# Gated linear attention and a multiplicative feed-forward block: state, scores and values of a chunk in one block of 64x64 quarters

## The chip, the cores and the metric

The kernel runs on one core of one Trainium2 chip. The metric is the device time of one execution in microseconds (us); the time of a kernel is the median of several runs. A profile is one further execution, with its own time; its span, from the first to the last instruction, is what the trace divides.

## The reference

For each of 4 batches and 8 heads, a state of 48x48 is decayed row by row and added to, token by token; q reads it. The result, 3072 tokens by 384, goes through a feed-forward block whose two gates are multiplied.

```python
batch, n_heads, seq, head_dim = (4, 8, 768, 48)
state = np.zeros((B, H, D, D), dtype=np.float32)
for t in range(S):
    state = alpha[:, :, t, :, None] * state + np.einsum('bhd,bhe->bhde', k[:, :, t], v[:, :, t])
    y[:, :, t] = np.einsum('bhd,bhde->bhe', q[:, :, t], state)
...
x = np.ascontiguousarray(attn_out.transpose(0, 2, 1, 3)).reshape(B * S, H * D)
a = x @ w1
b = x @ w2
h = a * b @ w3
return (h @ w_out).astype(np.float32)
```

w1 and w2 are 384x1024, w3 is 1024x1024, w_out 1024x384. These four weights arrive in 64-bit floats and are taken apart on the chip.

## The kernel before, in words

**Chunks.** The 768 tokens of a batch are 6 chunks of 128 (C), so there are 24 chunks in all (N) and chunk n is the first of its batch where n % 6 is 0. A loop over n from 0 to 24 has one step for each chunk and one more. It is software-pipelined: step n transposes chunk n + 1, computes the scores of chunk n, finishes the output of chunk n - 1, decays chunk n + 2 and takes logarithms for chunk n + 4.

**One chunk.** `logs` takes the logarithm of alpha (ScalarE). `decays` (L333) sums it over the tokens by a matmul with a triangular matrix and takes two exponentials, the tile `e`. `decayed` (L357) multiplies k and q by them (VectorE, tile `qk`). `transposed` (L370) turns `qk` on TensorE, and ScalarE copies it to `qkT`, with head 2j + i of a pair j on the 64 partitions of half i. `scores` (L446) multiplies k by q within a chunk, and VectorE masks them with a bitwise and against the upper triangle (L457) into `ms`. The output y of a chunk is the state times q (`attend_state`, L463) plus the values times the masked scores (`attend`, L477). ScalarE copies y to the tile `x` (L489), which SyncE stores to DRAM (`xd`), two transfers a chunk (`store`, L301, L305). `outer` (L386) forms k times v for the state, and `advance` (L405) decays the state every second chunk on GpSimd (T, L412). The decay factors get to T by way of DRAM: GpSimd's queue stores single rows of `e` (`ends`, L352 and L354) and loads them back with values on partitions (`load_ends`, L362, tile `dec`).

**Quarters.** A matmul with at most 64 rows and at most 64 columns of weights uses one 64x64 quarter of TensorE's array; four such run beside each other. From chunk 8 on (`TURNED`, L81) `turned_scores` (L422) leaves out the part of the scores that the mask removes: per pair and half one matmul of 64 keys by 128 queries and one of 64 by 64. For that, half i = 1 keeps its keys in exchanged halves, and the values must be exchanged too: `turn_v` (L164, two copies on GpSimd, L167) writes `vt`. The first 64 queries' values (`attend_low`, L415) of chunk n - 1 go between the scores of chunk n; the other 64 queries' (L482) follow after the transposes, with all 128 rows. Chunks 0 to 7 use the plain form: L454 for the scores, L485 for the values. In both, the two halves i write banks of their own (`sc[i]`, `y[i]`).

**Around it.** Three chunks make a group g of 384 tokens. `load_x` loads a group's x from `xd`, `split_x` (L503) splits it into three parts on ScalarE (L507) and VectorE (L508, L509), and `gate` makes one of 8 column tiles of a times b by 18 matmuls per factor (L515), in fp32r. Gates of groups 0 to 4 fill up the steps from 6 on. Weights w1 and w2 are converted (`to_fp32`, L226) in the same steps. After the loop the other gates, the product of w3 with w_out and the final projection follow.

**Order.** The framework schedules each engine's instructions by the order of the program, with `after_marks` holding back what follows until a marked instruction has been issued. SyncE's queue issues the loads of alpha, k, q, v and weights and the stores of x and of the gates (L590) in one order; before the change, `store` stands first in a step from step 6 on. v of chunks 3 to 7 is loaded by GpSimd's queue (L159).

Of the kernel before, what the change touches and what calls it, by code (L numbers as in the profile page):

```python
# [12 lines left out]
I32 = mybir.dt.int32  # L13
# [35 lines left out]
def kernel(  # L49
# [31 lines left out]
    TURNED = 8  # L81
# [79 lines left out]
    def turned(n):  # L161
        return TURNED <= n < N

    def turn_v(n):  # L164
        if turned(n):
            for half in range(2):
                nc.gpsimd.tensor_copy(out=vts[n % 2][ds(DP * half, DP), :, 0:D],  # L167
                                      in_=st["v", n][ds(DP * (1 - half), DP), 1::2, 0:D])
# [19 lines left out]
    made = work.tile([C, 2, NP, C], FP32, tag="ms", name="ms")  # L188
    utri, after = made[:, 0, 0, :], made[:, 0, 1, :]
# [3 lines left out]
    keep = p1.tile([C, C], I32, name="keep")  # L193
    keep_turned = p1.tile([C, 2, DP], I32, name="keep_turned")
# [11 lines left out]
    nc.vector.tensor_scalar_mul(keep, utri, -1.0)  # L206
    keep_bc = keep[:, None, :].to_broadcast([C, NP, C])
    for half in range(2):
        nc.gpsimd.tensor_copy(out=keep_turned[ds(DP * half, DP), 1 - half], in_=keep[ds(DP * half, DP), ds(DP * half, DP)])
    nc.gpsimd.memset(keep_turned[DP:, 1], -1)  # L210
# [122 lines left out]
    def decays(n):  # L333
# [17 lines left out]
        if n in ends:  # L351
            mark["pool"] = nc.gpsimd.dma_start(out=ends[n][0:1], in_=e[0:1, 0]).ins  # L352
        if n + 1 in ends:
            mark["pool"] = nc.gpsimd.dma_start(out=ends[n + 1][1:2], in_=e[C - 1:C, 1]).ins  # L354
        load_ends(n)
# [6 lines left out]
    def load_ends(n):  # L362
        if n not in ends:
            return
        with nc.allow_non_contiguous_dma(reason="single values to partitions"):
            for i in range(2):
                nc.gpsimd.dma_start(out=decs[n // 2 % 2][ds(DP * i, D)].rearrange("d m j -> d (m j)"),
                                    in_=ends[n].rearrange("m (j i d) -> i d (m j)", i=2, d=D)[i])
# [36 lines left out]
    def advance(n):  # L405
# [4 lines left out]
        nc.gpsimd.tensor_mul(dec, d[:, 0, :], d[:, 1, :])  # L410
# [4 lines left out]
    def attend_low(n, jj, i, half):  # L415

        s, w = ds(DP * i, DP), (vts[n % 2] if i else st["v", n])
        h = half * NP // 2 + jj
        nc.tensor.matmul(st["y", n][0][i][ds(DP * half, DP), jj, 0:DP], w[s, h if i else 2 * h, :],  # L419
                         st["ms", n][s, i, h, 0:DP], start=(n % NCH == 0 and jj == 0), stop=True, skip_group_check=True)  # L420

    def turned_scores(n):  # L422

        qkT = st["qkT", n]
        sc = [bank().rearrange("p (j c) -> p j c", j=NP) for _ in range(2)]
        for j in range(NP):
            for part in range(2):
                for i in range(2):
                    r, t = ds(DP * i, D), slice(DP * part, C)
                    nc.tensor.matmul(sc[i][ds(DP * (part ^ i), DP), j, t], qkT[r, 0, j, ds(DP * part, DP)],  # L430
                                     qkT[r, 1, j, t], start=True, stop=True)
            if turned(n - 1):
                for i in range(2):
                    attend_low(n - 1, j % 2, i, i ^ (j < 2))
        ms = work.tile([C, 2, NP, C], FP32, tag="ms", name="ms")
        for i in range(2):
            r = ds(DP * i, DP)
            low, high = (keep_turned[r, 0], keep_turned[:, 1]) if i else (keep[r, 0:DP], keep[:, DP:])
            for x, mask, t in ((slice(DP * i, DP * (i + 1)), low, slice(0, DP)), (slice(0, C), high, slice(DP, C))):
                masked = nc.vector.tensor_tensor(ms[x, i, :, t].bitcast(I32), sc[i][x, :, t].bitcast(I32),  # L440
                                                 mask[:, None, :].to_broadcast([x.stop - x.start, NP, DP]),
                                                 op=ALU.bitwise_and)
        ends_of_part1[0] = mark["ms", n] = masked.ins
        st["ms", n] = ms

    def scores(n):  # L446
        if turned(n):
            return turned_scores(n)
        qkT = st["qkT", n]
        sc = [bank().rearrange("p (j c) -> p j c", j=NP) for _ in range(2)]  # L450
        for j in range(NP):
            for i in range(2):
                r = ds(DP * i, D)
                nc.tensor.matmul(sc[i][:, j, :], qkT[r, 0, j, :], qkT[r, 1, j, :], start=True, stop=True)  # L454
        ms = work.tile([C, 2, NP, C], FP32, tag="ms", name="ms")
        for i in range(2):
            masked = nc.vector.tensor_tensor(ms[:, i].bitcast(I32), sc[i].bitcast(I32), keep_bc, op=ALU.bitwise_and)  # L457
        ends_of_part1[0] = mark["ms", n] = masked.ins
        st["ms", n] = ms

    HP = NP // 2

    def attend_state(n):  # L463
        qkT = st.pop(("qkT", n))

# [221 lines left out]
    for n in range(N + 1):  # L689
        if not 1 < n < FIRST:  # L690
            store()
# [185 lines left out]
```

## Time and profile before

| | us |
|---|---|
| median of 3 runs (463.63 to 465.16) | 464.42 |
| the profiled execution | 464.49 |
| its span | 462.8 |
| loop over chunks, with what precedes it | 0 to 184.6 |
| first gate matmul (L515) | 57.7 |
| after the loop | 184.6 to 462.8 |
| TensorE busy | 446.9 |
| VectorE busy | 371.7 |
| ScalarE busy | 276.4 |
| GpSimd busy | 95.1 |
| granted TensorE clock | 1.000 |

In the page and the trace, PE is TensorE's matmul, PEld its weight loads, DVE VectorE, ACT ScalarE, POOL GpSimd and SP SyncE; a q after a name is that engine's queue of DMA issues. L12 is line 12 of the kernel. A line of the timeline has the start, the time until the last of the merged instructions ended, the engine, the line, what is written and read, the shape and the count; in brackets stands the idle time ahead of it and who ended it. A line of a group has the busy time in all, the mean of one in ns, and the idle time ahead with its releasers. One fp32 matmul is two instructions. Ends of matmuls are modelled and overlap their successors, so differences of starts are used.

### The profile page before, as it was taken

How to read it: one execution, taken by the hardware profiler on the slowest of the kernel's cores; microseconds unless marked ns; L12 is line 12 of the kernel's file. 1: busy time of each engine (PE TensorE's matmuls, PEld its weight loads, DVE VectorE, ACT ScalarE, POOL GpSimd, SP SyncE). 2: the span in 40 equal slices, each digit the busy share in tenths (PEclk: the TensorE clock that was granted, in tenths of full speed). 3: DMA queues.
4: the chain of work that ended last, by engine and by line, in shares of the span. 5: the costliest groups of instructions: out<-in, count | busy, mean ns of one | idle time of the engine just before them, and what ended most of it. 6: DMA issues, size and time to landing. Idle time of an engine off the chain costs nothing.

```text
span 462.8 us, 11150 instructions
## 1 busy us (share of the span) xinstructions
PE 446.9 (97%) x4296; PEld 423.2 (91%) x4296; DVE 371.7 (80%) x610; ACT 276.4 (60%) x544; POOL 95.1 (21%) x186
## 2 busy tenths in 40 slices
PE   4998999999999999999999999999999999999996
PEld 2675699898999989999999999999999999999996
DVE  2779997999979988999998999997542967776671
ACT  4685975767658563988875676764545443333430
POOL 6234232325414430121221201212010000000000
PEclk9999999999999999999999999999999999999999
DMA  9999999999999974466856446412115875665511
GB/s 173 254 208 228 261 224 192 248 209 219 184 227 193 234 165 138 130 224 212 235 178 196 146 128 177 149 52 86 51 48 153 243 210 180 186 178 159 166 51 52
DMA packets 148869, 80.37 MB, mean 174 GB/s; under 512 B 97392, under 2 KB 138608, under 8 KB 148816
## 3 DMA queue, kind: packets, MB, share of 16 engines
q1 hardware_dynamic: 143040, 64.44, 57.3%
q0 software_dynamic: 5776, 15.22, 11.0%
q8 instruction: 34, 0.56, 0.5%
q14 instruction: 19, 0.16, 0.1%
HBM read 57.58 MB, written 22.06 MB: 172 GB/s over the span
## 4 chain that ended last, share of the span: by engine, by line
PE 88%; DVE 4%; DMA 4%; ACT 2%; issue 1%; SPq 0%; DVEq 0%; ACTq 0%
PE bank L515 72%; DMA kq<-in_q_dram 3%; PE bank L381 3%; PE bank L430 3%; PE bank L482 2%; PE bank L474 2%; PE bank L340 1%; PE bank L393 1%; PE bank L346 1%; PE bank L454 1%; PE bank L343 1%; PE bank L419 1%; DVE qk L359 1%; DVE ms L457 1%; PE bank L485 1%
## 5 line engine op out<-in xcount | busy, mean ns | idle before, releaser
L515 PE MATMUL bank<-x,w 128*128 128x384 f32 x1152 | 210.2, 337 | 1.7 <-ACT qkT L383 1.1
L515 PEld LDWEIGHTS bank<-x,w 128*128 128x128 f32 x1152 | 200.2, 188 | 4.1 <-ACT qkT L383 1.4
L515 PE MATMUL bank<-w3o,ab 128*128 128x384 f32 x576 | 100.2, 336 | 0.0
L515 PEld LDWEIGHTS bank<-w3o,ab 128*128 128x128 f32 x576 | 99.9, 188 | 0.0
L540 ACT ACTIVATE bank<-bank 128x384 f32<-128x384 f32 x96 | 45.6, 476 | 43.4 <-PE bank L515 43.1
L524 ACT ACTIVATE t<-bank 128x384 f32<-128x384 f32 x64 | 31.9, 499 | 54.9 <-PE bank L515 54.9
L590 POOL DMA_DIRECT2D abd<-ab x45 | 25.8, 573 | 137.9 <-DVE ab L576 121.3
L383 ACT COPY qkT<-bank 128x512 f32<-128x512 f32 x48 | 26.2, 596 | 24.8 <-PE bank L381 24.8
L641 DVE TENSOR_TENSOR ab<-abl,ab 128x1024 fp32r<-128x1024 f32 x24 | 29.3, 1223 | 12.3 <-ACT ab L640 12.3
L640 ACT ACTIVATE ab<-abl 128x1024 fp32r<-128x1024 f32 x24 | 25.5, 1061 | 20.2 <-PE bank L515 18.4
L515 PE MATMUL bank<-wo,w3T 128*128 128x384 f32 x192 | 35.9, 334 | 0.0
L576 DVE TENSOR_TENSOR ab<-bank,r 128x384 f32<-128x384 f32 x44 | 24.1, 548 | 12.5 <-PE bank L515 6.3
L515 PEld LDWEIGHTS bank<-wo,w3T 128*128 128x128 f32 x192 | 33.5, 188 | 0.0
L249 ACT ACTIVATE power<-power,rebias 128x512 uint32<-128x512 uint32 (+1 forms) x36 | 25.3, 701 | 12.6 <-DVE power L248 12.4
L359 DVE TENSOR_TENSOR qk<-kq,e 128x768 f32<-128x768 f32 x24 | 23.1, 964 | 11.3 <-ACT e L350 7.9
L526 DVE SCALAR_TENSOR_TENSOR o<-bank,t 128x384 f32<-128x384 f32 x24 | 13.4, 557 | 23.0 <-issue 13.7
L642 DVE SCALAR_TENSOR_TENSOR ab<-ab,abl 128x1024 fp32r<-128x1024 f32 x24 | 29.2, 1217 | 0.0
L526 DVE SCALAR_TENSOR_TENSOR r<-bank,t 128x384 f32<-128x384 f32 x40 | 22.0, 550 | 6.8 <-PE bank L515 3.4
L251 DVE SCALAR_TENSOR_TENSOR mant<-mant,rest 128x512 f32<-128x512 uint32 (+1 forms) x36 | 23.4, 649 | 3.7 <-ACT rest L244 3.7
L252 DVE SCALAR_TENSOR_TENSOR power<-raw,power 128x512 uint32<-128x512 uint32 (+1 forms) x36 | 23.5, 653 | 2.4 <-ACT power L249 2.4
L253 DVE TENSOR_TENSOR mant<-mant,power 128x512 f32<-128x512 f32 (+1 forms) x36 | 23.6, 655 | 0.5
L244 ACT ACTIVATE rest<-raw 128x512 f32<-128x512 uint32 (+1 forms) x36 | 23.3, 649 | 0.0
(102 smaller groups left out, 675.2 us busy)
## 6 DMA issues: line engine op xcount, KB each, us to landing
abl<-abd SPq DMA_DIRECT2D x24, 512.0 KB, 4.7
abd<-ab POOLq DMA_DIRECT2D x45, 192.0 KB, 3.2
raw<-in_moe_w_dram SPq DMA_DIRECT2D x64, 128.0 KB, 3.4
raw<-in_moe_w_dram SPq DMA_DIRECT2D x12, 512.0 KB, 5.8
xT<-xd POOLq DMA_DIRECT2D x9, 576.0 KB, 4.7
kq<-in_k_dram SPq DMA_DIRECT2D x24, 192.0 KB, 5.2
kq<-in_q_dram SPq DMA_DIRECT2D x24, 192.0 KB, 5.4
xd<-x SPq DMA_DIRECT2D x48, 96.0 KB, 3.9
```

The source lines that it names most:

```text
L249: nc.scalar.activation(power, power, AF.Relu, scale=2.0 ** 23, bias=rebias)
L359: mark["qk", n] = nc.vector.tensor_mul(qks[n % 3][:, :, :, 0:D], st.pop(("kq", n)), st.pop(("e", n)).rearrange("p i (h d) -> p i h d", h=H ...
L383: mark["qkT", n] = nc.scalar.copy(qkT[:, :, :, ds(DP * half, DP)], tp[half]).ins
L515: nc.tensor.matmul(p, w[part][i], x[part][i], start=start and part == parts[0] and i == 0, stop=stop and part == parts[-1] and i == n - 1, ...
L524: nc.scalar.activation(t, p1, AF.Copy, scale=(1.0 + 1.0 / P) * scale)
L526: nc.vector.scalar_tensor_tensor(to, p2, scale, t, op0=ALU.mult, op1=ALU.add)
L540: nc.scalar.activation(p, p, AF.Copy, scale=1.0 + 1.0 / P)
L576: nc.vector.tensor_mul(ab, p, r[0])
L590: (nc.gpsimd if late else nc.sync).dma_start(out=abd[g][:, f, :], in_=ab)
L640: nc.scalar.activation(t[:, 0], ab, AF.Copy, scale=1.0 - 2.0 ** -13)
L641: nc.vector.tensor_sub(t[:, 1], ab, t[:, 0].bitcast(FP32))
L642: nc.vector.scalar_tensor_tensor(t[:, 2], t[:, 0].bitcast(FP32), -1.0 - 1.0 / P, ab, op0=ALU.mult, op1=ALU.add)
```

## The change

- State, scores and values of a step become one block, `attention` (L471 of the new kernel), with two streams of matmuls. One stream uses the off-diagonal quarters and writes one bank: state, values of the first 64 keys and values of the last 64 keys for the heads of pairs 0 to 2 (LQ = 3). The other uses the diagonal quarters: all scores of chunk n, and then pair 3 of chunk n - 1, in a bank of its own. The streams are interleaved by a count of columns.
- All chunks take this form, chunks 0 to 7 too, so all get the exchange `vt`, now of all values that the off-diagonal and diagonal quarters need.
- The scores lie in two banks by queries and keys, and two masks of 512 and 256 columns take the place of four (two in chunks 0 to 7). `keep` becomes one tile with a half of ones.
- y lies in two banks of three pairs and one pair: ScalarE's two copies are of 384 and 128 columns instead of 256 each, and x is stored in four transfers a chunk instead of two.
- On GpSimd, `turn_v` comes ahead of `advance`, and the transfers of the decays and T's products wait for it by a mark. `load_ends` moves from `decays` of step n to behind `advance` of the next step.
- From step 6 on `store` follows the loads of k, q and v, so that `load_x` is first in its step. `logs(4)` waits for the copies of y.

```diff
     def turn_v(n):
-        if turned(n):
-            for half in range(2):
-                nc.gpsimd.tensor_copy(out=vts[n % 2][ds(DP * half, DP), :, 0:D],
-                                      in_=st["v", n][ds(DP * (1 - half), DP), 1::2, 0:D])
+        if n < N:
+            for i in range(2):
+                mark["vt"] = nc.gpsimd.tensor_copy(out=vts[n % 2][ds(DP * i, DP), :, 0:D],
+                                                   in_=st["v", n][ds(DP * (1 - i), DP), i::2, 0:D]).ins
...
-        if n in ends:
-            mark["pool"] = nc.gpsimd.dma_start(out=ends[n][0:1], in_=e[0:1, 0]).ins
-        if n + 1 in ends:
-            mark["pool"] = nc.gpsimd.dma_start(out=ends[n + 1][1:2], in_=e[C - 1:C, 1]).ins
-        load_ends(n)
+        with after_marks("vt"):
+            if n in ends:
+                mark["pool"] = nc.gpsimd.dma_start(out=ends[n][0:1], in_=e[0:1, 0]).ins
+            if n + 1 in ends:
+                mark["pool"] = nc.gpsimd.dma_start(out=ends[n + 1][1:2], in_=e[C - 1:C, 1]).ins
...
+    def attend(n):
+        ms, vc, vt, qkT = st.pop(("ms", n)), st.pop(("v", n)), vts[n % 2], st.pop(("qkT", n))
+        y = [bank()[:, 0:x * C].rearrange("p (j c) -> p j c", c=C) for x in (LQ, NP - LQ)]
+        first, state = set(), n % NCH > 0
+        def add(j, i, w, x, t):
+            at = j >= LQ
+            to = y[at][ds(DP * (i if at else 1 - i), DP), j - LQ * at, t]
+            nc.tensor.matmul(to, w, x, start=(at, i) not in first, stop=True, skip_group_check=True)
+            first.add((at, i))
+        def steps(heads):
+            for j in heads * state:
+                yield 2, [(j, i, Ts[n % 2][ds(DP * i, D), j, :], qkT[ds(DP * i, D), 1, j, :], slice(0, C)) for i in range(2)]
+            for j in heads:
+                yield 2, [(j, i, vt[DP:, j, :] if i else vc[0:DP, 2 * j, :], ms[ds(DP * i, DP), 0:2, j, :], slice(0, C))
+                          for i in range(2)]
+            for j in heads:
+                yield 1, [(j, i, vc[DP:, 2 * j + 1, :] if i else vt[0:DP, j, :], ms[ds(DP * i, DP), 2, j, :], slice(DP, C))
+                          for i in range(2)]
...
+        def copied():
+            x = work.tile([C, NP, C], FP32, tag="x", name="x", bufs=4)
+            for a, b in zip(y, (x[:, 0:LQ], x[:, LQ:])):
+                mark["x"] = ends_of_part1[1] = nc.scalar.copy(b, a).ins
...
+            for half in range(2):
+                s = ds(DP * half, D)
+                later.append((to[1 - half, :, 0:LQ], x[s, 0:LQ]))
+                later.append((to[half, :, LQ:], x[s, LQ:]))
...
+    def scores(n):
+        qkT = st["qkT", n]
+        sc = [bank().rearrange("p (e j c) -> p e j c", e=2, j=NP), bank()[:, 0:NP * DP].rearrange("p (j c) -> p j c", j=NP)]
+        def score(x):
+            j, late = x
+            for i in range(2):
+                r, to = ds(DP * i, D), ds(DP * i, DP)
+                q = qkT[r, 1, j, ds(DP * late, DP)] if late else qkT[r, 1, j, :].rearrange("p (e c) -> p e c", e=2)
+                nc.tensor.matmul(sc[1][to, j, :] if late else sc[0][to, :, j, :], qkT[r, 0, j, ds(DP * late, DP)], q,
+                                 start=True, stop=True)
+        def masked():
+            ms = st["ms", n] = work.tile([C, 3, NP, DP], FP32, tag="ms", name="ms")
+            for x, y, keep in ((ms[:, 0:2], sc[0], keep_bc[1]), (ms[:, 2:], sc[1][:, None], keep_bc[0])):
+                last = nc.vector.tensor_tensor(x.bitcast(I32), y.bitcast(I32), keep, op=ALU.bitwise_and)
...
+    def attention(n):
+        low, high = attend(n - 1) if n else ([], [])
+        done = None
+        if n < N:
+            own, done = scores(n)
+            high = own + high
+        low, high, at = deque(low), deque(high), [0, 0]
+        while low or high:
+            k = 0 if not high or low and at[0] <= at[1] else 1
+            cost, f, x = (low, high)[k].popleft()
+            at[k] += cost
+            f(x)
...
     for n in range(N + 1):
-        if not 1 < n < FIRST:
+        if n < 2:
             store()
...
         if n >= FIRST:
             load_v(n + 2)
-        if n:
-            attend_state(n - 1)
-        if n < N:
-            scores(n)
...
+            store()
+        attention(n)
         transposed(n + 1)
...
+        if n:
+            turn_v(n)
         advance(n)
-        turn_v(n)
+        if n > 1:
+            load_ends(n + 2)
+        elif n == 1:
+            load_ends(2)
         if n:
-            attend(n - 1)
+            st.pop(("x", n - 1))()
+        if n == 1:
+            with after_marks("x"):
+                logs(4)
         outer(n)
```

## The prediction

> **What bounds the kernel now.** I read the page's chain and engine shares first, then the 40 slices, then time by stage, TensorE's timeline through single steps, and the groups by shape.
>
> ```profile
> PE 446.9 (97%) x4296; PEld 423.2 (91%) x4296; DVE 371.7 (80%) x610; ACT 276.4 (60%) x544; POOL 95.1 (21%) x186
> ...
> PE 88%; DVE 4%; DMA 4%; ACT 2%; issue 1%; SPq 0%; DVEq 0%; ACTq 0%
> ```
>
> TensorE (PE) is the chain. But the share hides three stages. From 0 to 57.7 us the DMA engines are full (their share lies between 0.96 and 1.19 in every stretch) and the chain holds two q transfers of 7.4 and 7.1 us. From 57.7 to 184.6 us (steps 7 to 24 of the loop over chunks) TensorE is nearly contiguous, idle about 2.2 us, and DVE is almost as full (8.02 of 8.10 us between 91.0 and 99.1). From 184.6 us on nothing of the change runs: 278.2 us stay.
>
> So the stage to price is the middle one. One of its steps, step 12, on TensorE:
>
> ```profile
> 99.12 0.67 PE L474 MATMUL bank<-qkT,T 48*64 48x128 f32 x16
> ...
> 99.61 0.38 PE L430 MATMUL bank<-qkT 48*64 48x128 f32 x7
> ...
> 100.83 0.71 PE L381 MATMUL bank<-ident,qk 64*128 64x64 f32 x16
> ...
> 101.47 0.34 PE L482 MATMUL bank<-ms,v 128*64 128x64 f32 x4
> ...
> 101.98 0.62 PE L393 MATMUL bank<-v,qk 128*64 128x48 f32 x16
> ```
>
> Take starts, not durations, which overlap. State: 99.12 to 99.61, 0.49 us. Scores with the low half of the values: 99.61 to 100.83, 1.22 us. High half of the values: 101.47 to 101.98, 0.51 us. Attention is 2.22 us of the step.
>
> A measure makes old and new comparable. Call one matmul of 64 columns on one 64x64 quarter one unit. State is 8 matmuls of 128 columns over four quarters, 4 units each: 0.49/4 = 0.122 us. The scores' block loads the diagonal quarters with 10 units and the others with 6: 1.22/10 = 0.122, so the fuller pair sets the time. The high half spans all rows: 4 units on each column half, 0.128. Together 18 units.
>
> **Part 1, the block of quarters.** It has the same multiplications. The off-diagonal pair gets pairs 0 to 2: 3 x (2+2+1) = 15 units; the diagonal pair gets the scores, 4 x 3 = 12, and pair 3, 5: 17. At 0.122 that is 2.07 us, 0.15 less than 2.22. After a batch's first chunk, without state, the old step is 1.22 + 0.51 = 1.73 and the new one 15 units, 1.83: 0.10 more. Step 24, without scores, took 1.50 (183.14 to 184.64) and needs 15 units, 1.83: 0.33 more. Step 8 pays 1.47 + 0.92 = 2.39 now and 2.07 then: -0.32. Sum over steps 8 to 24: 13 x -0.15 - 0.32 + 2 x 0.10 + 0.33 = **-1.74 us** if TensorE alone decided.
>
> It doesn't where groups change (steps 9/10, 13/14, 17/18, 21/22), which have too little gate work to cover a latency:
>
> ```profile
> 79.04 1.07 ACT L383 COPY qkT<-bank 128x512 f32<-128x512 f32 x2 [2.18 <-PE bank L381]
> ...
> 80.00 1.18 ACT L507 ACTIVATE x<-xT 128x1152 fp32r<-128x1152 f32 x1
> ...
> 82.48 1.50 DVE L509 SCALAR_TENSOR_TENSOR x<-x,xT 128x1152 fp32r<-128x1152 f32 x1
> ...
> 85.14 0.72 ACT L249 ACTIVATE power<-power,rebias 128x512 uint32<-128x512 uint32 x1 [1.26 <-DVE power L248]
> ...
> 86.39 2.37 PE L515 MATMUL bank<-x,w 128*128 128x384 f32 x12 [1.10 <-ACT qkT L383]
> ```
>
> Here the end is set by ACT's copy of qkT, ACT's split of x, DVE's split and a conversion, then ACT's next qkT copy. The change ends attention 2.07 us into the step where transposes started at 1.71, and puts the copies of y (now 384 and 128 columns, about 0.49 + 0.29 by the 384-column and 256-column rows; before 0.65) ahead of qkT. So this chain starts about 0.4 us later, and that step pair's gain (together -0.95) may vanish: between -0.95 and +0.6. I take -0.45, half.
>
> **Part 2, the masks.** Four instructions become two.
>
> ```profile
> L457 DVE TENSOR_TENSOR ms<-bank,keep 128x512 int32<-128x512 int32 x16 | 10.3, 682 | 0.7 <-PE bank L454 0.5
> ...
> L440 DVE TENSOR_TENSOR ms<-bank,keep_turned 64x256 int32<-64x256 int32 x16 | 6.8, 428 | 0.5
> L440 DVE TENSOR_TENSOR ms<-bank,keep_turned 128x256 int32<-128x256 int32 x16 | 6.8, 425 | 0.2
> L440 DVE TENSOR_TENSOR ms<-bank,keep 64x256 int32<-64x256 int32 x16 | 6.5, 408 | 0.0
> L440 DVE TENSOR_TENSOR ms<-bank,keep 128x256 int32<-128x256 int32 x16 | 6.5, 406 | 0.0
> ```
>
> From 1.667 to 0.682 + 0.425 = 1.107 us: 0.56 less in each of 16 steps, 9 us of DVE, and 0.26 less in each of the first eight. DVE is not the chain, so only TensorE's small waits shrink: about 2.2 us idle plus some 1 us of stretched gates (L515 x18 took 3.68 at 93.56 where 3.39 is usual). Between 0 and -1.5; I take -0.5.
>
> **Part 3, GpSimd.** Chunks 0 to 7 get the exchange too: 16 more copies x 0.557 = 8.9 us, in a stage where POOL is busy 22 of 57.7 us. They now stand ahead of the decays' transfers and of T. What queues behind a copy that waits for v (4.66 us at worst) are those transfers, T, and, through the double-buffered e, ACT's Exp two steps on. The shortest two steps last 8 us, so this is hidden; uncovered it would cost a few tenths at T. Against it, the load of the decays leaves POOL's queue one step later, where it no longer blocks (17.2 us of POOL waits for the decays' stores), and T of step 4 should come earlier (TensorE waited 0.83 for it). In the early stage none of that counts unless transfers come sooner. Its last 8 us (49.4 to 57.7) are TensorE's: step 6 goes from 0.60 + 1.09 + 0.92 to 2.07, a wait of 0.4 us for a copy of y disappears, but chunk 6's values move ahead of the first gate. Between -1.0 and +1.0; I take -0.3.
>
> By "SBUF — State Buffer", section Who interferes with whom, a DVE instruction with two SBUF inputs and a GpSimd one reading SBUF exclude each other. The copies agree (407 ns median, 1377 at worst); by the rule the 16 new ones would each hold DVE up to one copy, an estimate of 6.5 us of DVE in the early stage, which a full DMA would partly cover.
>
> **Part 4, SyncE.** x leaves in four transfers a chunk instead of two; packets and bytes stay.
>
> ```profile
> L305 SPq DMA_DIRECT2D xd<-x x48: 303/443/2842, 29.5 to 185.6; - x48
> ```
>
> Two more issues are 0.89 us a step. SP's rows lie end to end from 64 to 130 us, but much is back pressure (q: 0.57 at least, 1.40 median) and waiting for other engines (about 6 us between 58 and 100, 25 between 100 and 185). From step 6 on k, q and v go ahead of the stores, which gives back two stores in the order. Between 0 and +3; I take +0.2.
>
> **Sum.** -1.74 without the transitions' -0.95 is -0.79; -0.45; -0.5; -0.3; +0.2: -1.8 us. The profiled execution took 464.49 (span 462.8), 0.07 above the median: 462.7 for it, **462.6** as a median.
>
> **Rivals.** (B) No change: the transitions take back more than half, say +0.2 each beyond zero, the masks' relief goes into DVE idleness and the early stage stays with its transfers: -0.79 + 0.8 + 0, about 464.4. For it: four chains through ACT that get no shorter. Against it: eight steps with long gates that hide ACT.
>
> (D) The early stage moves as well: it loses 8 x 0.26 us on DVE, TensorE's waits for T (0.83) and for y's copies (0.4 + 0.3), some 2 us more: 460.6. Against it: DMA share above 1 there.
>
> (C) Slower, by SyncE's queue: v of chunk 10 is issued at 76.85 and lands near 82.2, and the outer product needs it at 83.42, 1.2 us of room. Eight steps of 0.89 us are 7.1 us against some 6 us of waiting that can absorb them. If v lands more than 1.2 us later there, each of four transitions and the steps beside them lose 0.5 to 1 us: +4 on A, 466.5.
>
> (E) The two row halves of a quarter pair serialize. In the old block each row half writes a bank of its own; in the new one both write halves of one bank, which no row shows. Then 34 units, 4.1 us a step: +2.07 x 17 = +35, about 498. Against it: state rows already put two column halves into one bank at full rate.
>
> "TensorEngine Tiling (Array Packing)", Gotcha 1: PSUM Pressure, speaks against this change: different row tiles, it says, can't access one PSUM bank simultaneously. By it the sum is E's, by the state rows A's.
>
> **Numbers.** A 0.38, B 0.30, C 0.15, D 0.12, E 0.05. Faster by over 0.3% (1.4 us, about what a measurement can tell from no change): A and D, 0.50. Within: B, 0.30. Slower: C and E, 0.20. The range takes A, B and D with their ends, 460.4 to 465.8, and leaves out C and E.
>
> **What would show it.** Right: a stateful step has 2.05 to 2.15 us from its first state matmul to the transposes; masks about 1.1 us; steps 8 to 24 span about 115 us instead of 116.9; the first gate still starts near 57.7. Wrong: attention of 4 us (E); L393 waiting for v (C); TensorE's gaps at the group changes above 1.1 us (B); the first gate before 56 us (D).

## The result and the profile after

The changed kernel takes **475.55 us** (median of 4 runs, 474.72 to 477.53) against 464.51 in the same rounds: the ratio is 1.0245 (95% interval 1.0208 to 1.0282), 11 us slower. The prediction said 462.6.

The page of the changed kernel, with the shares of the engines, two rows of the 40 slices and the chain:

```profile
PE 447.4 (95%) x4552; PEld 426.0 (90%) x4552; DVE 361.5 (76%) x580; ACT 277.8 (59%) x544; POOL 105.9 (22%) x199
...
PE   4988899797999999999999999999999999999996
...
PEclk9989899999899999999999999999999999999999
...
PE 72%; DMA 11%; DVE 6%; SPq 5%; ACT 3%; issue 3%; DVEq 0%; ACTq 0%
```

TensorE is busy as long as before (447.4 against 446.9 us), but in a span of 473.2 instead of 462.8. Its share of the chain fell from 88% to 72%; DMA rose from 4% to 11%, and SyncE's queue, at 0% before, is on it with 5%. And PEclk, which was full throughout, has three slices of 8 among the nines: the clock that TensorE was granted is 0.989 over the span, where before had 1.000.

Three marks split the 10.4 us of span. The first gate's matmul stands at 61.19 us instead of 57.68 (+3.5). From there to the last transposes (those of chunk 23, in step 22) it is 117.24 us instead of 110.67 (+6.6). From there to the end, 294.8 instead of 294.4 (+0.4). So the early stage lost a third and the middle stage two thirds.

**How SyncE's queue gets to TensorE.** SyncE's rows of the changed kernel around the change from group 1 to group 2:

```profile
104.31 0.36 SPq L489 DMA_DIRECT2D xT<-xd  x1
...
106.10 3.52 SPq L159 DMA_DIRECT2D v<-in_v_dram  x1
109.67 2.11 SPq L300 DMA_DIRECT2D xd<-x  x4
111.88 0.85 SPq L578 DMA_DIRECT2D abd<-ab  x2
```

v's row lasts 3.52 us; behind it come four stores of x, and only then, at 111.88, the stores of two gates' products. Then the timeline of all engines (in brackets the idle time ahead of a row and what ended it):

```profile
115.52 0.56 DVE L551 TENSOR_TENSOR ab<-r 128x384 f32<-128x384 f32 x1 [3.67 <-DMA abd<-ab]
...
116.86 1.01 DVE L466 TENSOR_TENSOR ms<-bank,keep 128x512 int32<-128x512 int32 x2
...
117.60 0.27 PE L460 MATMUL bank<-qkT 48*64 48x64 f32 x2 [2.74 <-DVE ms L466]
```

VectorE has stood 3.67 us for the buffer of a product whose store came last; the masks stand behind it, and TensorE waits 2.74 us for them. An earlier place, in the chain of waits:

```profile
72.67 0.60 SPq L159
73.32 2.25 SPq L300
75.62 0.43 SPq L300
76.09 0.44 SPq L300
76.58 2.16 DMA xd<-x
78.75 4.34 DMA xT<-xd
```

Here x's load of a group (L489) is issued only at 78.75, against 72.08 in the profile before: x's last stores stand immediately ahead of it in the queue, and the load needs them in DRAM. By itself this place costs little: ScalarE's split of x, next in that chain, waits 0.33 us for the load at 83.11.

**And the clock.** Time by windows of 3.41 us in the same trace. The columns after the length are the busy time of PE, PEld, DVE, ACT and POOL with their counts, then the granted clock, the DMA share and GB/s:

```profile
26.91:30.32 3.41, 1.27 (x29) 0.83 (x31) 2.40 (x5) 2.01 (x4) 1.80 (x5) 1.00 1.11 268
30.32:33.73 3.41, 3.41 (x78) 3.29 (x70) 1.57 (x3) 3.00 (x7) 2.78 (x5) 0.50 1.12 159
47.39:50.80 3.41, 1.91 (x12) 1.01 (x16) 2.36 (x5) 3.00 (x7) 2.73 (x4) 1.00 0.96 174
50.80:54.21 3.41, 3.41 (x75) 3.41 (x75) 3.19 (x7) 2.36 (x6) 0.50 (x1) 0.50 0.79 155
115.65:119.06 3.41, 1.46 (x62) 1.46 (x64) 3.41 (x6) 1.79 (x5) 0.00 (x0) 1.00 1.12 207
119.06:122.47 3.41, 3.41 (x46) 3.08 (x41) 3.41 (x6) 1.89 (x5) 1.78 (x5) 0.50 0.80 232
```

The lines come in pairs. In the first of a pair TensorE is idle for 2.14, 1.50 and 1.95 us (3.41 less the first column); in the second it is busy throughout, at a clock of 0.50. So each of these waits costs its own length and, as an estimate from half of 3.41 us at half clock, up to 1.7 us more.

The masks did what was forecast. In the groups by shape:

```profile
L466 DVE TENSOR_TENSOR ms<-bank,keep 128x512 int32<-128x512 int32 x24 | 16.3, 681 | 0.7 <-PE bank L460 0.7
...
L466 DVE TENSOR_TENSOR ms<-bank,keep 128x256 int32<-128x256 int32 x24 | 9.9, 412 | 0.0
```

### The profile page after: what moved, and what is told of

The parts are those of the page before. It is cut to its first block, busy times and chain, and to the rows that moved or that the text cites. A ratio compares the mean times of both kernels' runs of the same rounds, so it can differ in the third digit from the quotient of the medians.

```text
span 473.2 us, 11711 instructions
## 1 busy us (share of the span) xinstructions
PE 447.4 (95%) x4552; PEld 426.0 (90%) x4552; DVE 361.5 (76%) x580; ACT 277.8 (59%) x544; POOL 105.9 (22%) x199
## 4 chain that ended last, share of the span: by engine, by line
PE 72%; DMA 11%; DVE 6%; SPq 5%; ACT 3%; issue 3%; DVEq 0%; ACTq 0%
PE bank L503 62%; DMA kq<-in_q_dram 3%; SPq L300 3%; PE bank L420 3%; DMA xT<-xd 2%; PE bank L376 2%; PE bank L460 2%; DMA raw<-in_moe_w_out_dram 2%; DMA abd<-ab 2%; DVE qk L354 2%; DMA ac<-in_alpha_dram 2%; PE bank L388 1%; SPq L231 1%; DMA xd<-x 1%; PE bank L335 1%
## 5 line engine op out<-in xcount | busy, mean ns | idle before, releaser
L512 ACT ACTIVATE t<-bank 128x384 f32<-128x384 f32 x64 | 30.9, 489 | 52.4 <-PE bank L503 51.1
L460 PE MATMUL bank<-qkT 48*64 48x128 f32 (+1 forms) x768 | 40.8, 259 | 2.7 <-DVE ms L466 2.7
L460 PEld LDWEIGHTS bank<-qkT 48*64 48x64 f32 x768 | 37.0, 143 | 4.4 <-DVE ms L466 3.0
L420 PE MATMUL bank<-ms,v 64*64 64x64 f32 (+1 forms) x384 | 39.6, 255 | 1.4 <-issue 1.2
L420 PEld LDWEIGHTS bank<-ms,v 64*64 64x64 f32 x384 | 36.9, 141 | 2.7 <-issue 1.9
L164 POOL COPY vt<-v 64x192 f32<-64x192 f32 x48 | 27.5, 574 | 51.5 <-DMA v<-in_v_dram 49.8
L420 PE MATMUL bank<-ms,vt 64*64 64x64 f32 (+1 forms) x384 | 38.9, 255 | 0.0
L420 PEld LDWEIGHTS bank<-ms,vt 64*64 64x64 f32 x384 | 36.5, 141 | 0.0
L354 DVE TENSOR_TENSOR qk<-kq,e 128x768 f32<-128x768 f32 x24 | 23.0, 957 | 13.8 <-ACT e L345 8.2
```

The source lines that it names most:

```text
L164: mark["vt"] = nc.gpsimd.tensor_copy(out=vts[n % 2][ds(DP * i, DP), :, 0:D], in_=st["v", n][ds(DP * (1 - i), DP), i::2, 0:D]).ins
L354: mark["qk", n] = nc.vector.tensor_mul(qks[n % 3][:, :, :, 0:D], st.pop(("kq", n)), st.pop(("e", n)).rearrange("p i (h d) -> p i h d", h=H ...
L420: nc.tensor.matmul(to, w, x, start=(at, i) not in first, stop=True, skip_group_check=True)
L460: nc.tensor.matmul(sc[1][to, j, :] if late else sc[0][to, :, j, :], qkT[r, 0, j, ds(DP * late, DP)], q, start=True, stop=True)
L512: nc.scalar.activation(t, p1, AF.Copy, scale=(1.0 + 1.0 / P) * scale)
```

## The experiments

All times are medians; the ratio is to the kernel before in the same rounds, with its 95% interval. **Q** stands for SyncE's queue. Of the traces I use the first gate's start, the time from there to the last transposes, those of chunk 23 (the middle stage), and the number of windows of 3.41 us at half clock. These marks come from one profile each. Run 8 has the code of before up to its last stage, and its first gate stands at 58.76 us instead of 57.68; run 9 differs from step 6 on only, and has 56.91. So a difference of 1 us in that mark shows nothing.

**1. Two stores a chunk.** ScalarE puts pair 3 into the rows of the other half, so one transfer fits.

```diff
-            for a, b in zip(y, (x[:, 0:LQ], x[:, LQ:])):
-                mark["x"] = ends_of_part1[1] = nc.scalar.copy(b, a).ins
+            nc.scalar.copy(x[:, 0:LQ], y[0])
+            for half in range(2):
+                mark["x"] = ends_of_part1[1] = nc.scalar.copy(x[ds(DP * (1 - half), DP), LQ:], y[1][ds(DP * half, DP)]).ins
...
-                later.append((to[1 - half, :, 0:LQ], x[s, 0:LQ]))
-                later.append((to[half, :, LQ:], x[s, LQ:]))
+                later.append((to[1 - half], x[s]))
```

> The changed kernel, but x leaves in two transfers a chunk, as before: ACT copies pair 3 out of PSUM in two pieces of 64 partitions, each into the rows of the other half, so that one transfer fits each half (one more ACT copy a chunk). All else as changed. Theory N (the number of stores): two issues more a chunk fill SyncE's queue, loads and stores of the gates' products come late, and TensorE's waits behind them let the granted clock drop; then most of the 11.0 us come back: 464 to 468 us, clock 1.00. Theory P (their place behind the loads): little changes, 473 to 476 us. Theory G (GpSimd's order) and theory B (the block itself draws the clock down): 474 to 476 us, clock 0.98 to 0.99.

Measured: 471.53 us, ratio 1.0150 (1.0111 to 1.0190). 4.0 us come back, less than theory N asked and more than the others allowed. Number is a part, not the whole.

**2. The stores' old place.**

```diff
-        if n < 2:
+        if not 1 < n < FIRST:
             store()
...
             load_v(n + 2)
-            store()
```

> The changed kernel, but from step 6 on x's four stores are issued at the head of the step again, ahead of x's load and of the loads of k, q and v. Theory P: the wait of x's load for stores issued just before it (xT was issued at 78.75 us instead of 72.08) and of the gates' products for free buffers go; 466 to 470 us. Theory N: four issues cost the same wherever they stand, 474 to 478 us. Theories G and B: 474 to 476 us.

Measured: 472.48 us, ratio 1.0172 (1.0136 to 1.0208): 3.1 us back, less than theory P asked and more than the others allowed.

**3. GpSimd's old order.**

```diff
-        if n:
-            turn_v(n)
         advance(n)
-        if n > 1:
-            load_ends(n + 2)
-        elif n == 1:
-            load_ends(2)
+        if n:
+            turn_v(n)
```

(and `load_ends(n)` at the end of `decays` again, without the marks "vt")

> The changed kernel, but on GpSimd the decays' transfers and T's product stand ahead of v's exchange again, and the decays are loaded in the step that made them; chunks 0 to 7 keep their exchange. Theory G: the first gate comes at 57 to 58 us instead of 61.2, and 3 to 4 us come back in the early stage, 471 to 472 us, with no half clock before 57 us. Theories N and P: 474 to 476 us, first gate still near 61 us. Theory B: 475 us, clock still 0.98 to 0.99.

Measured: 475.26 us, ratio 1.0217 (1.0167 to 1.0268). The first gate moved to 59.08, about half of what theory G asked, and the middle stage took 121.06 us with three windows at half clock: in all nothing came back.

**4. All three.**

> The changed kernel with all three edits: two stores a chunk, issued at the head of the step, and GpSimd's old order. What is left of the change is the block of quarters, its two masks and the exchange for chunks 0 to 7. If the block is worth what the prediction gave it (part 1 and 2, -1.7 us) and the loss is the queues', 461 to 464 us at clock 1.00. Theory B (64x64 quarters themselves draw the clock down): clock stays at 0.98 to 0.99 and the time at 469 us or more.

Measured: 463.84 us, ratio 0.9989 (0.9965 to 1.0014). The three edits give 11.7 us together and 7.4 when their single effects are added. The middle stage is 109.79 us, 0.9 less than before. One window at half clock remains.

**5. Both edits to Q, GpSimd as changed.** Edits 1 and 2.

> The changed kernel with both edits to SyncE's queue (two stores a chunk, issued at the head of the step) and GpSimd's new order left as changed. It asks how much of the 11.7 us between the changed kernel and the one with all three edits back is GpSimd's. Alone the edits gave 4.0 (number), 3.1 (place) and 0.3 us (GpSimd). Theory S (SyncE's queue is the whole loss; its two edits do together what neither does alone): 463 to 465 us. Theory G2 (GpSimd's order matters once the queue is mended): 467 to 469 us.

Measured: 465.26 us, ratio 1.0020 (0.9995 to 1.0044). Against before in the same rounds 1.2 us of the loss are left, and the interval holds none: some 9.9 of the 11.0 us are Q's two edits, against 7.1 for the two alone. The time is 0.3 us above the range of theory S and 1.7 below that of theory G2. The block runs as planned here; its start and the transposes that follow, in the timeline of step 12:

```profile
98.59 0.33 PE L420 MATMUL bank<-qkT,T 48*64 48x128 f32 x2
98.61 0.33 PE L460 MATMUL bank<-qkT 48*64 48x128 f32 x2
...
99.30 0.27 PE L420 MATMUL bank<-ms,v 64*64 64x128 f32 x1
99.31 0.27 PE L420 MATMUL bank<-ms,vt 64*64 64x128 f32 x1
...
100.50 0.22 PE L420 MATMUL bank<-ms,v 64*64 64x64 f32 x1
100.65 0.71 PE L376 MATMUL bank<-ident,qk 64*128 64x64 f32 x16
```

From 98.59 to 100.65 are 2.06 us, where the prediction had 2.07. The middle stage of this profile takes 109.07 us; the profile, 462.88 us, is the fastest of the ten runs, and seven of the other nine have a clock below 1.000.

**6. T first, then the exchange.** Edit 5, and v's load of chunks 3 to 7 behind the exchange.

```diff
+        advance(n)
         if n:
             turn_v(n)
-        advance(n)
+        if n < FIRST:
+            with after_marks("vt"):
+                load_v(n + 2)
```

> The changed kernel with both edits to SyncE's queue, and on GpSimd T's product first, then v's exchange, then the load of the next v and the decays' transfers. With all three edits back TensorE stood from 30 to 32.5 us for v's exchange, behind transfers that GpSimd issued first, and ran at half clock from 32 to 35.7; in the changed kernel it stood from 27.5 to 29.7 for T behind the exchange, and ran at half clock from 30.3 to 33.7. If these stalls and what the clock makes of them cost the early stage 1.3 us (first gate at 58.95 instead of 57.68), this order gives 462 to 463 us, clock 1.00, first gate near 57.7. If the early stage is set by its transfers anyway: 463.5 to 464.5.

Measured: 465.12 us, ratio 1.0025 (1.0004 to 1.0047); first gate at 59.06. Another stall took the place of the old one (2.15 us idle in the window from 33.0, half clock from 36.4). No order of GpSimd's gains clearly: the old one (run 4), the new one (run 5) and this one stand at 0.9989, 1.0020 and 1.0025, with intervals that overlap.

**7. Before, with the new queue.** Nothing of the change but this:

```diff
-        if not 1 < n < FIRST:
+        if n < 2:
             store()
...
             load_v(n + 2)
+            store()
...
-            later.append((to[half, :, :, ds(c * C, C)], x[ds(DP * half, D)]))
+            for h in (slice(0, 3), slice(3, 4)):
+                later.append((to[half, :, h, ds(c * C, C)], x[ds(DP * half, D), h]))
```

> The kernel before, with only the two edits to SyncE's queue that the change makes: four stores a chunk, and from step 6 on behind the loads of k, q and v, x's load ahead of them. No block of quarters, no new copies. If the queue is the loss by itself: 468 to 472 us, with TensorE idle in stretches of 2 us and half clock behind them. If it takes the block (TensorE earlier, or its 64x64 quarters drawing the clock down): 464 to 466 us, clock 1.00.

Measured: 477.16 us, ratio 1.0289 (1.0244 to 1.0333): 13.1 us lost, with no block and no new copy, more than the 4 to 8 expected. The queue makes the loss by itself. Its rows in that trace:

```profile
77.44 0.58 SPq L154 DMA_DIRECT2D kq<-in_q_dram  x1
78.12 2.60 SPq L159 DMA_DIRECT2D v<-in_v_dram  x1
80.77 3.54 SPq L305 DMA_DIRECT2D xd<-x  x4
...
84.89 0.85 SPq L591 DMA_DIRECT2D abd<-ab  x2
85.84 0.45 SPq L147 DMA_DIRECT2D ac<-in_alpha_dram  x1
```

Four stores take 3.54 us here, and products and alpha stand behind them. Who waits, in us in all, times and longest:

```profile
POOL vt L167 <- DMA v<-in_v_dram: 31.6, 9, 7.3
...
ACT la L324 <- DMA ac<-in_alpha_dram: 6.9, 4, 3.2
```

**8. Pauses.** The kernel before, with TensorE held up in the last stage.

```diff
+        if n in PROBE:
+            pause = lastp.tile([C, DM], FP32, tag="pause", name="pause", bufs=1)
+            nc.vector.tensor_copy(out=pause, in_=o)
+            for _ in range(PROBE[n]):
+                nc.vector.tensor_scalar_mul(pause, pause, 1.0)
+            nc.tensor.matmul(bank()[:, 0:DP], pause[:, 0:C], pause[:, 0:DP], start=True, stop=True)
```

> The kernel before, with TensorE held up seven times in the last stage, where it is otherwise contiguous: after the rows of chunks 2, 5, 8, 11, 14, 17 and 20 a small extra product waits for a chain on DVE (a copy and 0, 2, 4, 6, 3, 8 and 5 more passes over 128x384), estimated at 1.0, 1.7, 2.4, 3.1, 2.0, 3.8 and 2.7 us of idleness from DVE's 0.55 us for o and about 0.35 us for a pass. No 64x64 products are near. Theory W (a wait of TensorE makes the clock drop): the granted clock falls to one half for some 3 us after the pauses of 2 us and more, not after 1.0. Theory B (64x64 quarters draw it down): 1.00 throughout.

Measured: one run, 513.62 us. The pauses were longer than estimated, 1.30 us and then 2.90 to 6.28; the two shortest:

```profile
373.68 0.41 PE L656 MATMUL bank<-pause 128*128 128x64 f32 x2 [1.30 <-DVE pause L653]
...
389.53 0.69 PE L656 MATMUL bank<-pause 128*128 128x64 f32 x2 [2.90 <-DVE pause L655]
```

And the clock by windows around these two (columns as above):

```profile
371.59:375.00 3.41, 2.10 (x13) 1.81 (x12) 2.55 (x5) 1.06 (x1) 0.00 (x0) 1.00 0.96 281
375.00:378.40 3.40, 3.40 (x22) 3.40 (x21) 0.86 (x1) 0.55 (x2) 0.00 (x0) 1.00 0.55 170
385.25:388.66 3.41, 1.38 (x8) 1.06 (x7) 2.57 (x5) 1.55 (x2) 0.00 (x0) 1.00 0.50 149
388.66:392.07 3.41, 2.54 (x9) 2.54 (x10) 1.95 (x3) 0.00 (x0) 0.00 (x0) 0.50 0.42 138
392.07:395.48 3.41, 3.41 (x12) 3.41 (x11) 0.00 (x0) 0.00 (x0) 0.00 (x0) 0.50 0.56 155
395.48:398.90 3.42, 3.42 (x21) 3.42 (x21) 1.41 (x2) 1.55 (x2) 0.00 (x0) 1.00 0.14 51
```

After 1.30 us the clock stays at 1.00. After 2.90 us, of which 2.03 lie in one window, it is 0.50 for two windows, in a stretch of 128x128 matmuls. All six longer pauses did this, the first did not. Theory W holds: a wait of 2.90 us or more halves the clock, one of 1.30 does not. In the changed kernel it is a consequence of waits, not a cost of the quarters: the profile of kernel 5 ran its quarters at 1.000.

**9 and 10. Place alone and number alone, on the kernel before.** The two halves of edit 7.

> The kernel before, with x's two stores a chunk moved behind the loads of k, q and v from step 6 on, and x's load first in its step. With four stores as well it took 477.2 us, 13.1 more than before. If place alone does it: 475 us or more. If place and number multiply, as the changed kernel suggests (4.0 and 3.1 us back alone, 10.3 together): 466 to 470 us.

> The kernel before, with x leaving in four transfers a chunk, pairs 0 to 2 and pair 3 apart, at the head of the step as before. If the number alone does it: 475 us or more. If place and number multiply: 466 to 470 us. If 0.89 us of issues a step find room in SyncE's waiting, as the prediction's sum had it: 464 to 465 us.

Measured: place 465.17 us, ratio 1.0019 (0.9992 to 1.0045); number 472.63 us, ratio 1.0195 (1.0141 to 1.0249). Place alone costs 0.9 us (the interval holds none), number alone 8.3, both 13.1. With two stores the place does hardly anything; with four it adds 4.7.

Number alone shows a shorter way from the queue to TensorE. In its trace 5.4 of the 6.2 us that the middle stage loses lie between the transposes of chunks 15 and 16:

```profile
112.18 1.21 SPq L159 DMA_DIRECT2D v<-in_v_dram  x1
...
117.75 1.10 PE L393 MATMUL bank<-v,qk 128*64 128x48 f32 x16 [2.89 <-DMA v<-in_v_dram]
```

v of chunk 14 is issued at 112.18 us, against 107.34 before, and the outer product waits 2.89 us for it. From 116.48, within this wait, to 123.31 the clock is 0.50.

**11 and 12. ScalarE's copies of y behind qkT's.** On kernel 5 and on kernel 4.

```diff
         if n:
-            st.pop(("x", n - 1))()
+            with after_marks(*[("qkT", n + 1)] * (n < N - 1)):
+                st.pop(("x", n - 1))()
```

> The changed kernel with both edits to SyncE's queue (465.3 us), and ACT copies y out of PSUM after its two copies of qkT instead of ahead of them. In that kernel the last chain ahead of the first gate (53.1 to 58.7 us) runs through 1.0 us of these copies; the transposes of step 8 stood at 57.20 there. If they are what the early stage and the changes of group still lose: 462.5 to 464 us, first gate at 58 us or before. If ACT's order costs nothing: 465.

> The kernel with all three edits back (463.8 us in its rounds), and ACT's copies of y after those of qkT. If ACT's order is worth 1 us: 462 to 463 us. If this kernel's remaining loss is the stall for v's exchange at 30 us and the half clock behind it: 463.5 to 464.5, clock 0.996.

Measured: 468.65 (1.0086, 1.0059 to 1.0113) and 468.34 us (1.0083, 1.0056 to 1.0109), 3.4 and 4.5 us slower than kernels 5 and 4 instead of 1 faster. TensorE's longest wait between 15 and 32 us in the first of them:

```profile
PE bank L335 <- ACT x L311: 3.5, 1, 3.5
```

L311 is the logarithm of chunks 4 and 5, which the change has behind y's copy in step 1: my edit moved it too. So these two alone can't tell the copies from the logarithm; runs 16 to 18 separate them.

**13. The stores on GpSimd.** The changed kernel, with `nc.gpsimd.dma_start` in `store`.

> The changed kernel with its four stores a chunk issued by GpSimd instead of SyncE, at the same places. Theory Q (SyncE's queue: what stands behind the stores there comes late): 464 to 467 us, x's load of the second group issued near 72 us again. Theory D (the traffic of four smaller transfers, whichever queue issues them): 472 to 476 us. A loss on GpSimd itself (v's exchange and T behind the issues) would show as TensorE's waits for T or vt.

Measured: 472.14 us, ratio 1.0159 (1.0121 to 1.0196), at the lower edge of theory D's range. The two stages go apart. The middle stage takes 113.19 us instead of 117.24, and x's load is issued at 72.18 again: 4.0 of the 6.6 us lost there go with SyncE's queue. But the first gate moved on to 62.52, and TensorE waits for T, which now stands behind GpSimd's issues (5.7 us of this ahead of the first gate, 2.1 in the changed kernel):

```profile
PE bank L420 <- POOL T L408: 7.3, 3, 4.5
```

The 2.5 us by which the middle stage is still above before could be traffic or GpSimd; this run can't say.

**14. Four buffers for the products.**

```diff
-    abp = pool("abp", 3)
+    abp = pool("abp", 4)
```

> The changed kernel with four buffers for the gates' products instead of three. DVE stood four times, 8.2 us in all, for a product's buffer whose store was queued behind x's stores; the longest, 3.7 us at 111.9, kept TensorE idle for 2.7 us and the clock at one half for 3.4 us. If that wait is the way by which the queue reaches TensorE in the middle stage: 470 to 472 us, no half clock at 119 us. If k, q, v and alpha are late as well: 474 to 476.

Measured: 480.99 us, ratio 1.0331 (1.0281 to 1.0380) against the changed kernel's 1.0245. VectorE's waits for a product's buffer are gone, but:

```profile
POOL vt L164 <- DMA v<-in_v_dram: 45.2, 9, 7.6
...
ACT la L319 <- DMA ac<-in_alpha_dram: 19.6, 9, 6.5
...
PE bank L388 <- DMA v<-in_v_dram: 9.2, 3, 5.3
```

In the changed kernel alpha kept ScalarE waiting 13.8 us in all, and TensorE's outer product (L388) never waited for v. My theory that the buffer is the way falls: SyncE issues the same transfers in the same order, and what TensorE waits for is another of them, v. Why the kernel is slower than with three buffers is not shown.

**15. The block from chunk 8 on only.** The kernel before, with the block, its two masks and the exchange of both halves for chunks 8 to 23, two stores a chunk at the old place, GpSimd's old order.

```diff
-        if n:
+        if n and not turned(n - 1):
             attend_state(n - 1)
-        if n < N:
+        if n < TURNED:
             scores(n)
         else:
-            for j in range(NP):
-                for i in range(2):
-                    attend_low(n - 1, j % 2, i, i ^ (j < 2))
+            attention(n)
```

> The kernel before, with the block of quarters, its two masks and the exchange of both halves from chunk 8 on only; chunks 0 to 7, SyncE's queue (two stores a chunk) and GpSimd's order as before. In the kernel with two stores at the old place, steps 8 to 24 took 110.5 us from the transposes of step 8 to those of step 23, against 111.3 before, and the early stage took 1 us more. If both add up: 462 to 463.5 us, first gate at 57.7. If the block gains nothing by itself: 464 to 465.

Measured: 464.00 us, ratio 0.9981 (0.9961 to 1.0000), clock 1.000, first gate at 56.68. That is a gain of a fifth of a per cent, and the interval reaches no change. (The expectation numbers the transposes by their chunk.)

**16 to 18. The logarithm and the copies, separated.** 16 is kernel 5 with the logarithm early; 17 is 16 with y's copies late; 18 is 17 with GpSimd's old order.

```diff
             decays(3)
             load_a(6)
+            with after_marks(("e", 3)):
+                logs(4)
...
-        if n == 1:
-            with after_marks("x"):
-                logs(4)
```

> The changed kernel with both edits to SyncE's queue (465.3 us), and the logarithm of chunks 4 and 5 right behind the exponential of chunk 3, as in the kernel before, instead of behind y's copy. y's copies stay ahead of qkT's. If the late logarithm costs the early stage its 1 us: 463.5 to 464.5, first gate near 57.7. If not: 465.

> The kernel with the early logarithm, and y's copies behind qkT's. If ACT's order costs what the prediction gave it (0.45 us at the changes of group) and some of the last chain ahead of the first gate: 462.5 to 464 us, below the run beside it. If the copies fit ahead of qkT anyway: the same as the run beside it. If the stall at 20.8 us was not the logarithm's: 468 again.

> As the run beside it, with GpSimd's old order as well. With the late copies and the late logarithm it stood at 468.3; without both at 463.8. If ACT's order gains: 462 to 463.5 us.

Measured: 463.31 us, ratio 0.9978 (0.9955 to 1.0002), first gate at 57.88; 467.37 us (1.0055, 1.0036 to 1.0075); 469.18 us (1.0106, 1.0068 to 1.0144). Kernel 16 stands at 0.9978 where kernel 5 has 1.0020, with intervals that overlap. It isn't shown that the logarithm does it: in the traces it starts at 22.33 us in run 16, at 22.13 in run 5 and at 19.72 in the changed kernel. Copies of y behind qkT's cost 4.1 us in the same rounds, with the logarithm early in both, so the logarithm was not the loss of runs 11 and 12. The profiles put this loss ahead of the first gate (+2.0) and behind the last transposes (+1.9); the middle stage takes 109.51 us against 109.35. Kernel 16 is the best found, and its interval still holds 1.

| kernel (its profiled execution) | first gate | middle stage | windows at half clock |
|---|---|---|---|
| before | 57.68 | 110.67 | 0 |
| changed | 61.19 | 117.24 | 3 |
| 1 two stores | 59.49 | 114.54 | 1 |
| 2 old place | 60.73 | 116.58 | 4 |
| 3 GpSimd's old order | 59.08 | 121.06 | 4 |
| 4 all three | 58.95 | 109.79 | 1 |
| 5 both edits to Q | 58.66 | 109.07 | 0 |
| 7 before, new queue | 59.84 | 120.17 | 5 |
| 9 before, new place | 56.91 | 111.48 | 0 |
| 10 before, four stores | 58.66 | 116.88 | 2 |
| 13 stores on GpSimd | 62.52 | 113.19 | 3 |
| 14 four buffers | 62.88 | 124.67 | 5 |
| 15 block from 8 | 56.68 | 112.07 | 0 |
| 16 early logarithm | 57.88 | 109.35 | 1 |

## Why the prediction was wrong

**The step that failed is part 4, SyncE**: "Between 0 and +3; I take +0.2". Runs 7, 9 and 10 put 13.1 us in its place, 8.3 for the number alone and 0.9 for the place alone.

What failed is the overlap, not the price. The price was a count times a median, 0.89 us a step. Where only the number changes it was about right: between 60 and 130 us x's stores take 10.9 us of SyncE's rows for 9 chunks in before (18 stores) and 18.7 for 9 chunks in run 10 (36 stores), 0.9 us a chunk more. In the changed kernel 32 stores take 21.8 us and in run 7 24.3, 1.5 to 1.8 us a chunk more. But with two stores at the new place (run 9) 16 take 14.5, 0.6 a chunk more, and the kernel hardly loses: a longer row is not by itself a longer time. The line that I showed had this spread in it, 303/443/2842; its kin after is

```profile
L300 SPq DMA_DIRECT2D xd<-x x96: 361/433/4704, 27.6 to 200.7; - x96
```

I read back pressure and SyncE's waits for other engines as room that absorbs more issues. Run 10 lost 8.3 us, more than the whole 7.1 that rival C's sum had for eight steps of 0.89. Nor could the rows have shown such room, or its lack: they fill 66.0 of the 70 us from 60 to 130 in before, 65.7 in the changed kernel, 65.3 in run 10, and 65.8 and 63.2 in runs 5 and 9, which lose about 1 us. "Which gives back two stores in the order" failed with it: what stands behind the stores in their new place is x's load of a group, the products' stores and the next step's alpha.

**Rival C** had this mechanism at a chance of 0.15, and too low a time, 466.5. I followed a single late transfer, v of chunk 10, with 1.2 us of room. Its sign, the outer product waiting for v, came in runs 10 (v of chunk 14) and 14, but not in the changed kernel, where x's load, a product's buffer and alpha were late. Run 14 showed that removing one of these waits saves nothing.

**What was left out altogether is the clock.** Every wait of TensorE was priced at its length. The three windows at half clock in the changed kernel are worth, as an estimate, up to 3 x 1.7 = 5.1 us, those in run 7 8.5. How much of that the early stage's transfers hide is not shown.

**Part 1's price was right.** In run 5 nine of steps 8 to 22 take 2.06 us for the block against 2.07, and step 13, after a batch's first chunk, 1.83 against 1.83. (In the prediction's reading of step 24 the bounds are 183.07 and 184.57 in the trace; the 1.50 us between them is right.) What the block is worth in the whole is not shown clear of noise. From the first gate to the end the profiles of runs 4, 5 and 16 are 2.1 to 2.7 us shorter than that of before, run 6 is 0.6 shorter and run 15 0.2 longer. The prediction had -1.2 for steps 8 to 24 with its half for the changes of group. Behind the last transposes all five are 1.1 to 1.3 us shorter, and there the copies of y count too: with them behind qkT's (run 17) that part is 0.8 us longer than before.

Rival E, the two row halves of a quarter pair serializing, did not come. The sentence of the Trainium skill that stood for it ("TensorEngine Tiling (Array Packing)", Gotcha 1: PSUM Pressure, which says that different row tiles can't access one bank at a time) is against the trace: rows of `vc` in one half and of `vt` in the other start 0.01 us apart at 99.30 and 99.31, in a block that writes one bank from both, each half to partitions of its own, and takes 2.06 us.

**Part 2 was right in size**: 681 + 412 ns against 682 + 425. Its worth of 0.5 us can't be told apart from part 1's.

**Part 3, GpSimd, stays open.** -0.3 was forecast; the first gate's mark reads +1.0 us in run 5 and +0.2 in run 16, within what that mark varies. The exchange, T and their order were worth nothing measurable: the old order changes -0.3 us in run 12 against 11 and +1.8 in run 18 against 17. The prediction has no word on the logarithm, though it stands in the diff; what that is worth is not shown either.

**The changes of group.** One of the two reasons that I gave for counting them at half, copies of y ahead of qkT, is not borne out: run 17 has them behind, and its middle stage, which holds all four changes, is no shorter (109.51 against 109.35 us).

So with the queue and the logarithm as before, the change measures 0.8 us faster (run 16, ratio 0.9978, 0.9955 to 1.0002), which can't be told from no change, where the sum without part 4 said 2.0.

**What stays open**: why a store of x holds SyncE for 0.5 to 0.9 us in groups of four where the shortest takes 0.36; whether the last 2.5 us of run 13 are the traffic of smaller transfers; and whether transfers, not issues, limit the middle stage. The DMA engines' share from 60 to 130 us is 1.02 in before, and the prediction called 0.96 to 1.19 full ahead of the first gate; it is 0.93 to 0.98 in the changed kernel and in runs 7 and 10. No run tests this.

## What to carry to other kernels

Before giving a DMA queue more to issue, don't count back pressure or waits in its rows as room: here 0.9 us a step more cost 8.3 us, where 0.2 was forecast. Don't read the cost from the sum of its rows either; look for the first transfer that an engine on the chain needs from behind them. Price a wait of TensorE at its length plus what the clock takes afterwards, once the idleness in 3.4 us comes near 1.5. And when a change bundles an engine's gain with a reordering, put the reordering alone on the old kernel first; here that one run (7) lost 13.1 us with nothing else of the change.

## What the runs showed of the hardware

**The clock falls in fixed windows.** Within each trace the granted clock falls to 0.5 at moments that are whole multiples of 3.413 us apart: 30.32, 50.80 and 119.06 us in the changed kernel (0, 6 and 26 windows), 388.66, 409.14, 429.62, 450.10, 470.58 and 491.06 with the pauses (6 windows each). Over the 20 traces from 8 us on, each window at full clock with 1.74 us or more of TensorE's idleness was followed by one at half clock, none with 1.46 or less was, and between them it went both ways (1.50, 1.59 and 1.61 were, 1.51, 1.63 and 1.73 were not). The idleness need not be in one piece: 1.50 us in the window from 47.39 were two waits. The half clock lasted one window or two. After a window at half clock that itself held 0.69 us or more of idleness a second one came each time (12 of 12); after one with 0.25 or less it came in 3 of 36.

The Trainium skill ("TensorE: Matmul & The Clock Gate", Part 1: The HAM clock gate) has the same free-running window, 3413 ns, and the clock of one half, but after at least one idle window. Here 1.74 idle microseconds within a window were always enough, and 1.50 once.

**Two queues fed by one order.** With two stores a chunk, moving them cost 0.9 us, which can't be told from nothing; with four, 4.7 us. SyncE's rows fill 63 to 66 of the 70 us from 60 to 130 in all four kernels, so their sum does not tell the two cases apart.
